# Retention in 64x64 array tiles, with the next chunk's scores inside a chunk's group and a second load of q

## The chip, the cores and the metric

One core of a Trainium2 chip runs the kernel. Its engines work side by side and wait for each other by semaphores: TensorE (PE in the profile; PEld is its loading of weights), VectorE (DVE), ScalarE (ACT), GpSimd (POOL) and SyncE (SP, which here issues the loads and stores). The metric is the device time of one execution in microseconds.

TensorE's array has 128 rows and 128 columns. A product uses as many rows as its contraction is long and as many columns as its weights have; the profile writes this shape as rows*columns. A product of 64 rows and 64 columns takes one of four such tiles, and which one follows from the partitions of its operands (rows) and of its output (columns). PSUM, where products land, has banks of 512 float32 per partition.

## What is computed

```
scores = q k^T / 8 ; ret = scores * gamma_h ** (t - s) for s <= t, else 0 ; x = ret v        # 8 batches, 8 heads, 576 tokens, 64 features a head
h = relu(x w_in) ; u, v = halves of h (512 + 512)
v_n = (v - mean) / sqrt(var + 1e-6) ; v_s = w_spatial v_n + b_spatial ; out = (u * v_s) w_out
```

The first line is the retention (the part that the change touches), the rest a gated feed-forward block that mixes the tokens with `w_spatial`.

## The kernel before

**Retention in chunks.** `retention(b)` is a generator for one batch. The 576 tokens are four chunks of 128 and a tail of 64 (chunk 4). Inside a chunk the decayed scores are applied directly; what earlier chunks contribute comes through a state of 64x64 per head. For a chunk c there are four kinds of float32 product, and in the profile each counts as two matmuls:

- `scores(c)`: k^T q per head. A pair of heads lies in the two halves of the partitions, so each product has 64 rows, 128 columns (all keys) and 128 queries: shape 64*128, named sc. DVE multiplies the result with the mask `am` (decay, and zero above the diagonal) into `at`.
- `burst(c)`, first part: the increments of the state (`ds`), k^T v for each half of the chunk: 64*64 with 64 moving columns, ox<-qkv in the profile.
- second part, for c > 0: the state times the decayed queries `qsc` (ox<-qsc,st), 64*64 with 128 columns.
- third part: `at` times v (ox<-at,qkv), contracting all 128 keys: 128*64 with 128 columns. It adds into the same output `xo` as the second part.

Then DVE adds the state's increments (`st`, with ACT's copy in chunk 0), POOL decays it by `sd`, ACT rounds `xo` to float32r (`hi`) and DVE takes the rest (`lo`): x is kept as two float32r parts, as all operands of the large products are.

**Preparation.** `prep(c)` is POOL's: k is scaled by `kd` in place, and q times `qs` goes to `qsc`. Both read the chunk's one load (`load`, 1 MB: q, k with features in partitions, k, v with tokens in partitions), issued two chunks ahead by SP after the group that frees its buffer.

**Order.** For each chunk: burst(c), load(c+2), prep(c+1), scores(c+1); a batch's first scores stand alone ahead of it. The pool `ps_r` gives scores and bursts, by turns, one of two pairs of PSUM banks.

**Main work.** The other products are float32r with 128 rows and 128 columns, three matmuls for each pair of two-part operands (`mm3`): v (512 columns), u, vs and f (288 columns). `main(b)` yields after each tile of output, and `interleave` puts a batch's retention between the tiles of the main work of the batch before, by shares that the generators yield. In the startup batch 0's retention runs with the conversion of the weights (`front`, `mid`, `back`, `w_sp_steps`, over ACT, DVE and POOL), in an order written out by hand; batch 1's retention lies in `main(0)`, together with the conversion of w_out (`convert_wout`). Up to there every engine keeps program order. After that (`ordered[0] = False`) a planner orders the instructions, except that the matmuls issued by `mm`, all of the retention's, keep their order. The `u_pair` tiles of batch 0 use the pairs of `ps_r` too.

Of the kernel before, what the change touches and what calls it, by code (L numbers as in the profile page):

```python
# [17 lines left out]
P = 128  # L18
# [12 lines left out]


@with_exitstack
def retention_gmlp(ctx, tc, qkv, qk_t, v_t, w_in, w_sp, b_sp, w_out, amask, qscale, kdec, sdec, out):
    nc = tc.nc
    cp = ctx.enter_context(tc.tile_pool(name="cp", bufs=1))
    ld = ctx.enter_context(tc.tile_pool(name="ld", bufs=2))
    wk = ctx.enter_context(tc.tile_pool(name="wk", bufs=2))
    sp = ctx.enter_context(tc.tile_pool(name="sp", bufs=1))
    ps_r = ctx.enter_context(tc.tile_pool(name="ps_r", bufs=2, space=PSUM))  # L40
    ps_m = ctx.enter_context(tc.tile_pool(name="ps_m", bufs=4, space=PSUM))

    am = cp.tile([P, 2, NP, C], F32, name="am")
# [12 lines left out]
        return cp.tile([P, 2, NCB, S], F32R, name=name, tag="slot", bufs=2)  # L56

    chunk = {}
    ordered = [True]

    class Engine:
# [28 lines left out]
    def spin(name, n):  # L90
        ps = ps_m.tile([P, 512], F32, name=name, tag="m")
        for i in range(n):
            pe.matmul(ps, idle[:, :P], idle, start=True, stop=True)

    spin("idle0", 12)

    def load(b, c):
        if b == 0 and c in (2, 3):
            tag = ("u", "wout0")[c - 2]
            t = cp.tile([P, NDB, S] if c == 2 else [P, NDB, DM], F32, name=f"qkv_{b}_{c}", tag=tag)  # L100
            t = t.rearrange("p a n -> p (a n)")[:, :4 * 512].rearrange("p (a n) -> p a n", a=4)
        else:
            t = ld.tile([P, 4, 512], F32, name=f"qkv_{b}_{c}", tag="qkv")
        q, k = (t[:, i].rearrange("p (a n) -> p a n", a=NP) for i in range(2))
        if c == NC:
            dma(t[:, :2].rearrange("p i (a n) -> p i a n", a=NP)[:, :, :, :TL], qk_t[b])
            for i in range(2):
                dma(t[i * TL:(i + 1) * TL, 3], v_t[b])
        elif (b, c) == (0, 0):
            dma(t[:, :2], qkv[b, c, :, :2])  # L110
            dma(am, amask)
            dma(kd, kdec)
            dma(t[:, 2:], qkv[b, c, :, 2:])
# [97 lines left out]
    def mm(out, w, r, start, stop):  # L211
        tc.keep_in_program_order(pe.matmul(out, w, r, start=start, stop=stop))

    def retention(b):
        at = {}
        qsc = {}
        half = [slice(i * D, (i + 1) * D) for i in range(2)]

        def rows(c):
            return C if c < NC else TL  # L220

        def scores(c):
            n = rows(c)
            q, k, _, _ = chunk[b, c]
            ps = ps_r.tile([P, 2, NP, C], F32, name=f"sc_{b}_{c}", tag="r")
            for p in range(NP):
                for i in range(2):
                    mm(ps[:n, i, p, :n] if c < NC else ps[half[i], i, p, :n], k[half[i], p, :n], q[half[i], p, :n], True, True)
            a = wk.tile([P, 2, NP, C], F32, name=f"at_{b}_{c}", tag="at")
            if c < NC:  # L230
                ve.tensor_tensor(out=a, in0=ps, in1=am, op=ALU.mult)
            else:
                for i in range(2):
                    r = half[i]
                    ve.tensor_tensor(out=a[r, i, :, :n], in0=ps[r, i, :, :n], in1=am[r, i, :, r], op=ALU.mult)
            at[c] = a

        def prep(c):
            q, _, kn, _ = chunk[b, c]
            n = rows(c)  # L240
            if c < NC:
                kh = kn.rearrange("p (h d) -> p h d", h=H)
                po.tensor_tensor(out=kh, in0=kh, in1=kd.broadcast_to([P, H, D]), op=ALU.mult)
            if c > 0:
                t = wk.tile([P, NP, C], F32, name=f"qsc_{b}_{c}", tag="qsc")
                po.tensor_tensor(out=t[:, :, :n], in0=q[:, :, :n], in1=qs[:, :, :n], op=ALU.mult)
                qsc[c] = t

        def burst(c):
            n = rows(c)  # L250
            _, _, kn, vv = chunk[b, c]
            ps = ps_r.tile([P, 2, 2, 2 * C], F32, name=f"ox_{b}_{c}", tag="r")
            ds = ps[:, :, 0].rearrange("p r (a d) -> p r a d", a=NP)
            xo = ps[:, :, 1].rearrange("p j (a n) -> p j a n", a=2)
            if c < NC:
                for p in range(NP):
                    for r in range(2):
                        for i in range(2):
                            m = i ^ r
                            hd = slice((2 * p + m) * D, (2 * p + m + 1) * D)  # L260
                            mm(ds[half[m], r, p], kn[half[r], hd], vv[half[r], hd], True, True)
            order = [(p, i) for j in range(2) for p, i in ((2 * j, 0), (2 * j, 1), (2 * j + 1, 1), (2 * j + 1, 0))]
            if c > 0:
                for p, i in order:
                    mm(xo[half[i ^ (p % 2)], i, p // 2, :n], st[c % 2][half[i], p], qsc[c][half[i], p, :n], p < 2, False)
            for p, i in order:
                h = 2 * p + i
                r = slice(0, n) if c < NC else half[i]
                mm(xo[half[i ^ (p % 2)], i, p // 2, :n], vv[r, h * D:(h + 1) * D], at[c][r, i, p, :n], c == 0, c == 0 or p >= 2)
            t = slice(c * C, c * C + n)  # L270
            hi, lo = ((xs[b][:, i, :, t] if c < NC else xt[:, :, i]).rearrange("p (a j) n -> p j a n", j=2) for i in range(2))
            src = xo[:, :, :, :n]
            if c < NC:
                new, tmp = st[(c + 1) % 2], st[2]
# [12 lines left out]

        xs[b] = slot(f"x_{b}")
        nxt = [(b, c) for c in range(NC + 1)] + [(b + 1, c) for c in range(2)]
        scores(0)  # L290
        yield 0.95
        prep(0)
        yield 0.0
        for c in range(NC + 1):
            yield from burst(c)
            if c + 2 < len(nxt) and nxt[c + 2][0] < B and nxt[c + 2] not in chunk:
                load(*nxt[c + 2])
            if c < NC:
                if b == 0:
                    yield 0.0  # L300
                prep(c + 1)
                if b == 0:
                    yield 0.0
                scores(c + 1)
            yield 2.65

    def mm3(ps, w, r, start, stop):
# [180 lines left out]
    up = {}  # L488

    def u_pair(db):  # L490
        t = ps_r.tile([P, 2, 512], F32, name=f"u_0_{db}", tag="r")
        up[db] = [t[:, i, :HALF] for i in range(2)]
        for i in range(2):
            u_mm(0, db, i, up[db][i])
# [55 lines left out]


_OUT = (B, DM, S)


def _constants():
# [5 lines left out]
    amask = np.where(rel[:, None, :] >= 0, scale * dec, 0.0)  # L561
    kdec = scale * gamma[None, :] ** (C - i)[:, None]
# [3 lines left out]
    f = lambda a: np.ascontiguousarray(a, dtype=np.float32)  # L566
    return {"amask": f(amask.reshape(C, NP, 2, C).transpose(0, 2, 1, 3)), "qscale": f(qscale), "kdec": f(kdec[..., None]), "sdec": f(sdec[..., None])}


def _layout(q, k, v, moe_w_in, moe_w_spatial, moe_b_spatial, moe_w_out):  # L570
# [10 lines left out]
        return a[..., :m].reshape(B, P, NP, NC, C).transpose(0, 3, 1, 2, 4).reshape(B, NC, P, NP * C)  # L581

    def tkc(a):
        return a[:, :m].reshape(B, NC, C, H * D)

    def heads(a):
        return a.reshape(H, D, -1)[[0, 2, 3, 1, 4, 6, 7, 5]].reshape(H * D, -1)

    c = np.ascontiguousarray
    return {  # L590
        "qkv": c(np.stack([fc(qf), fc(kf), tkc(kn), tkc(vv)], axis=3)),
        "qk_t": c(np.stack([qf[..., m:], kf[..., m:]], axis=2)),
        "v_t": c(vv[:, m:]),
        "w_in": c(heads(moe_w_in)).view(np.uint64),
        "w_sp": c(moe_w_spatial.T),
# [19 lines left out]
```

## Time and profile before

| | us |
|---|---|
| median of 3 runs | 577.2 |
| lowest, highest | 576.71, 577.96 |
| the profiled execution's own time | 577.02 |
| its span, first to last instruction | 574.9 |
| TensorE busy | 559.3 |
| VectorE busy | 273.3 |
| ScalarE busy | 208.4 |
| GpSimd busy | 126.9 |

The granted clock of TensorE was 0.99 on the mean. 56.60 MB were moved by DMA. The retention's products take 43.3 us (sc) and some 81 us (ox) of TensorE's busy time as the profile counts it; these lengths overlap where matmuls run in different tiles of the array, so the time that they occupy is read from where the next one starts. All code lines show as L69, the helper that records each operation, so groups are told apart by the names of their tiles.

### The profile page before, as it was taken

How to read it: one execution, taken by the hardware profiler on the slowest of the kernel's cores; microseconds unless marked ns; L12 is line 12 of the kernel's file. 1: busy time of each engine (PE TensorE's matmuls, PEld its weight loads, DVE VectorE, ACT ScalarE, POOL GpSimd, SP SyncE). 2: the span in 40 equal slices, each digit the busy share in tenths (PEclk: the TensorE clock that was granted, in tenths of full speed). 3: DMA queues.
4: the chain of work that ended last, by engine and by line, in shares of the span. 5: the costliest groups of instructions: out<-in, count | busy, mean ns of one | idle time of the engine just before them, and what ended most of it. 6: DMA issues, size and time to landing. Idle time of an engine off the chain costs nothing.

```text
span 574.9 us, 13265 instructions
## 1 busy us (share of the span) xinstructions
PE 559.3 (97%) x5716; PEld 510.6 (89%) x5716; DVE 273.3 (48%) x603; ACT 208.4 (36%) x451; POOL 126.9 (22%) x128
## 2 busy tenths in 40 slices
PE   7897997999999999999999999999999999999997
PEld 5677996989998899988999899998999889998997
DVE  5878667173532725157251654417353382515350
ACT  4365422264122632236222552226422362225422
POOL 4686555222001220122102220022201122000000
PEclk8999998999999999999999999999999999999999
DMA  8974222522133311432124221232213331010002
GB/s 328 368 242 138 74 77 63 204 75 74 38 114 118 91 63 42 182 108 79 38 74 157 74 75 38 95 136 74 75 38 124 107 112 59 16 63 21 2 1 83
DMA packets 29740, 56.60 MB, mean 98 GB/s; under 512 B 10737, under 2 KB 23025, under 8 KB 25714
## 3 DMA queue, kind: packets, MB, share of 16 engines
q1 hardware_dynamic: 29682, 55.76, 28.8%
q8 instruction: 45, 0.74, 0.5%
q14 instruction: 13, 0.11, 0.1%
HBM read 46.31 MB, written 9.44 MB: 97 GB/s over the span
## 4 chain that ended last, share of the span: by engine, by line
PE 85%; DVE 6%; POOL 3%; ACT 2%; issue 2%; DMA 1%; SPq 0%; ACTq 0%; POOLq 0%
PE vs L69 19%; PE f L69 17%; PE u L69 17%; PE v L69 16%; PE ox L69 10%; PE sc L69 6%; DVE f L69 2%; DMA raw_v<-in_w_in 1%; DVE w L69 1%; POOL f L69 1%; DVE at L69 1%; POOL qsc L69 1%; DVE st L69 1%; POOL qkv L69 1%; POOL wout L69 0%
## 5 line engine op out<-in xcount | busy, mean ns | idle before, releaser
L69 PE MATMUL vs<-wsp,vn 128*128 128x288 f32 x768 | 114.0, 297 | 0.0
L69 PE MATMUL u<-x,win 128*128 128x288 f32 x768 | 107.1, 299 | 3.2 <-POOL win L69 1.9
L69 PEld LDWEIGHTS u<-x,win 128*128 128x128 f32 x768 | 104.6, 191 | 5.3 <-POOL win L69 2.4
L69 PEld LDWEIGHTS vs<-wsp,vn 128*128 128x128 f32 x768 | 105.2, 188 | 1.6
L69 PE MATMUL f<-g,wout 128*128 128x288 f32 x768 | 105.4, 296 | 0.0
L69 PEld LDWEIGHTS f<-g,wout 128*128 128x128 f32 x768 | 102.7, 188 | 0.6
L69 PE MATMUL v<-win,x 128*128 128x512 f32 x384 | 94.1, 400 | 0.0
L69 PEld LDWEIGHTS v<-win,x 128*128 128x128 f32 x384 | 70.9, 188 | 17.8
L69 POOL TENSOR_TENSOR qkv<-qkv,kd 128x512 f32<-128x512 f32 x32 | 33.9, 1059 | 142.1 <-DMA qkv<-in_qkv 117.7
L69 DVE TENSOR_TENSOR at<-sc,am 128x1024 f32<-128x1024 f32 (+1 forms) x48 | 45.6, 950 | 40.4 <-PE sc L69 40.2
L69 ACT CAST g<-vs 128x288 fp32r<-128x288 f32 x64 | 25.5, 399 | 102.2 <-DVE vs L69 99.9
L69 DVE TENSOR_TENSOR st<-ox,st 128x256 f32<-128x256 f32 x56 | 23.5, 420 | 66.8 <-PE ox L69 65.5
L69 ACT COPY o<-f 128x288 f32<-128x288 f32 x64 | 25.5, 400 | 72.3 <-PE f L69 72.3
L69 POOL TENSOR_TENSOR st<-st,sd 128x256 f32<-128x256 f32 x24 | 14.7, 613 | 151.2 <-DVE st L69 151.2
L69 DVE BATCH_NORM_STATS2 s<-v 128x6 f32<-128x512 f32 (+1 forms) x40 | 27.9, 697 | 36.4 <-ACT v L69 35.5
L69 DVE TENSOR_TENSOR g<-vs,g 128x288 fp32r<-128x288 f32 x64 | 29.3, 457 | 30.3 <-ACT g L69 30.3
L69 PE MATMUL sc<-qkv 64*128 64x128 f32 (+1 forms) x640 | 43.3, 276 | 0.2 <-DMA qkv<-in_qkv 0.2
L69 PEld LDWEIGHTS sc<-qkv 64*128 64x128 f32 (+1 forms) x640 | 36.0, 180 | 7.9 <-issue 7.1
L69 DVE TENSOR_TENSOR vs<-vs,u 128x288 f32<-128x288 f32 x64 | 29.7, 464 | 26.6 <-PE vs L69 26.6
L69 ACT ACTIVATE u<-u 128x288 f32<-128x288 f32 x64 | 25.6, 407 | 44.6 <-PE u L69 44.6
L69 PE MATMUL ox<-at,qkv 128*64 128x128 f32 (+1 forms) x640 | 40.4, 274 | 0.1
L69 POOL TENSOR_TENSOR qsc<-qkv,qs 128x512 f32<-128x512 f32 (+1 forms) x32 | 36.7, 1148 | 12.0 <-DMA qkv<-in_qk_t 10.5
(64 smaller groups left out, 511.9 us busy)
## 6 DMA issues: line engine op xcount, KB each, us to landing
qkv<-in_qkv SPq DMA_DIRECT2D x31, 1024.0 KB, 5.1
out<-o SPq DMA_DIRECT2D x64, 144.0 KB, 1.8
raw_v<-in_w_in SPq DMA_DIRECT2D x4, 512.0 KB, 7.1
qkv<-in_qk_t SPq DMA_DIRECT2D x8, 256.0 KB, 3.3
qkv<-in_v_t SPq DMA_DIRECT2D x16, 128.0 KB, 3.3
raw<-in_w_in SPq DMA_DIRECT2D x4, 512.0 KB, 7.5
raw<-in_w_out SPq DMA_DIRECT2D x4, 512.0 KB, 3.4
raw_s<-in_w_sp SPq DMA_DIRECT2D x4, 288.0 KB, 8.4
```

The lines of the kernel that those rows point to most:

```text
L69: ins = op(*args, **kw)
```

## The change

- **Scores in blocks.** The products are cut by halves of the keys: the first 64 keys against all queries from there on, the second 64 keys only against the last 64 queries. Each has 64 rows and 64 columns. The block above the diagonal isn't computed; what the mask's operation reads there is left from earlier use of the bank. The two pairs of banks are cleared by memsets at the start.
- **at times v in two parts.** The first 64 queries contract 64 keys (64*64, 64 columns), the last 64 queries 128 keys (128*64, 64 columns).
- **Tiles of the array.** In odd pairs of heads the halves are exchanged (`side`): for `at`, the state, the decayed queries and the tokens of k and v of four heads (`_TURNED`). Host-side layouts and constants follow. The sequence `heads` lets four products in a row fall on the four 64x64 tiles, with the rows' half deciding the bank.
- **Order.** From batch 1 on scores(c+1) is issued inside burst(c), between the state's product and at's, and prep(c+1) ahead of the burst. The first scores of batches 2 to 7 are issued inside the tail's burst of the batch before. Batch 0 keeps its order.
- **Second load of q.** The decayed state needs q with exchanged halves, so `qsc` is loaded from an array of its own (`q_x`, 256 KB a chunk; `q_xt`, 128 KB for the tail) into its buffer right behind the chunk's load, and POOL scales it in place. In batch 0, chunk 3's uses the buffer of `vl`, and the tail's load comes after `fetch_wsp`.
- **PSUM.** The two pairs are two fixed tiles that `pair()` hands out by turns. The tail's mask is one operation instead of two.

```diff
+    banks = [ps_r.tile([P, 2, 512], F32, name=f"r{i}") for i in range(2)]
+    for t in banks:
+        ve.memset(t, 0.0)
...
+    def load_qsc(b, c):
+        t = wk.tile([P, NP, C], F32, name=f"qsc_{b}_{c}", tag="vl" if (b, c) == (0, 3) else "qsc", bufs=1 if (b, c) == (0, 3) else 2)
+        if c < NC:
+            dma(t, q_x[b, c - 1].rearrange("p (a n) -> p a n", a=NP))
+        else:
+            dma(t[:, :, :TL], q_xt[b])
+        qsc[b, c] = t
...
+    heads = [[(p, i) for p in (2 * j, 2 * j + 1) for i in range(2)] for j in range(NP // 2)]
+    heads = heads[0] + heads[1]
+
+    def side(p, i):
+        return i ^ (p % 2)
+
+    def scores(b, c):
+        n = rows(c)
+        q, k, _, _ = chunk[b, c]
+        ps = pair().rearrange("p i (a n) -> p i a n", a=NP)
+        for s in range(n // D):
+            for p, i in heads:
+                mm(ps[half[s ^ side(p, i)], i, p, s * D:n], k[half[i], p, half[s]], q[half[i], p, s * D:n], True, True)
+        a = wk.tile([P, 2, NP, C], F32, name=f"at_{b}_{c}", tag="at")
+        ve.tensor_tensor(out=a[:, :, :, :n], in0=ps[:, :, :, :n], in1=am[:, :, :, :n], op=ALU.mult)
+        at[b, c] = a
...
+        def burst(c, nx):
...
             if c > 0:
-                for p, i in order:
-                    mm(xo[half[i ^ (p % 2)], i, p // 2, :n], st[c % 2][half[i], p], qsc[c][half[i], p, :n], p < 2, False)
-            for p, i in order:
-                h = 2 * p + i
-                r = slice(0, n) if c < NC else half[i]
-                mm(xo[half[i ^ (p % 2)], i, p // 2, :n], vv[r, h * D:(h + 1) * D], at[c][r, i, p, :n], c == 0, c == 0 or p >= 2)
+                for p, i in heads:
+                    e = side(p, i)
+                    mm(xo[half[i], e, p // 2, :n], st[c % 2][half[e], p], qsc[b, c][half[e], p, :n], p < 2, False)
+            if b and nx:
+                scores(*nx)
+            for s in range(n // D):
+                for p, i in heads:
+                    h = 2 * p + i
+                    e = side(p, i)
+                    r = half[e] if s == 0 else slice(0, n)
+                    t = slice(s * D, (s + 1) * D)
+                    mm(xo[half[i], e, p // 2, t], vv[r, h * D:(h + 1) * D], at[b, c][r, i, p, t], c == 0 and s == 0 and p < 2, s == n // D - 1 and p >= 2)
...
         for c in range(NC + 1):
-            yield from burst(c)
+            nx = nxt[c + 1] if nxt[c + 1][0] < B else None
+            if b and nx:
+                prep(*nx)
+            yield from burst(c, nx)
             if c + 2 < len(nxt) and nxt[c + 2][0] < B and nxt[c + 2] not in chunk:
                 load(*nxt[c + 2])
```

More of the change, by code (lines that the diff above doesn't have):

```diff
@@ L33, in retention_gmlp @@
 @with_exitstack
-def retention_gmlp(ctx, tc, qkv, qk_t, v_t, w_in, w_sp, b_sp, w_out, amask, qscale, kdec, sdec, out):
+def retention_gmlp(ctx, tc, qkv, q_x, qk_t, q_xt, v_t, w_in, w_sp, b_sp, w_out, amask, qscale, kdec, sdec, out):
     nc = tc.nc
@@ L39, in retention_gmlp @@
     sp = ctx.enter_context(tc.tile_pool(name="sp", bufs=1))
-    ps_r = ctx.enter_context(tc.tile_pool(name="ps_r", bufs=2, space=PSUM))
+    ps_r = ctx.enter_context(tc.tile_pool(name="ps_r", bufs=1, space=PSUM))
     ps_m = ctx.enter_context(tc.tile_pool(name="ps_m", bufs=4, space=PSUM))
@@ L58, in retention_gmlp @@
     chunk = {}
+    qsc = {}
     ordered = [True]
@@ L93, in spin, with pair @@
             pe.matmul(ps, idle[:, :P], idle, start=True, stop=True)
-    spin("idle0", 12)
+    banks = [ps_r.tile([P, 2, 512], F32, name=f"r{i}") for i in range(2)]
+    for t in banks:
+        ve.memset(t, 0.0)
+    def pair():
+        banks.reverse()
+        return banks[0]
+    spin("idle0", 12)
+    def load_qsc(b, c):
[5 more added lines that the diff above has]
+        qsc[b, c] = t
     def load(b, c):
@@ L116, in load @@
         chunk[b, c] = q, k, t[:, 2], t[:, 3]
+        if c and (b, c) != (0, NC):
+            load_qsc(b, c)
     staged = {}
@@ L212, in mm @@
         tc.keep_in_program_order(pe.matmul(out, w, r, start=start, stop=stop))
-    def retention(b):
[L215 to L249, printed above, removed]
@@ new lines, in retention_gmlp, with rows @@
+    at = {}
+    half = [slice(i * D, (i + 1) * D) for i in range(2)]
+    def rows(c):
+        return C if c < NC else TL
+    heads = [[(p, i) for p in (2 * j, 2 * j + 1) for i in range(2)] for j in range(NP // 2)]
[12 more added lines that the diff above has]
+        at[b, c] = a
@@ L250, in burst, with prep @@
+    def prep(b, c):
+        n = rows(c)
+        if c < NC:
+            kh = chunk[b, c][2].rearrange("p (h d) -> p h d", h=H)
+            po.tensor_tensor(out=kh, in0=kh, in1=kd.broadcast_to([P, H, D]), op=ALU.mult)
+        if c > 0:
+            t = qsc[b, c][:, :, :n]
+            po.tensor_tensor(out=t, in0=t, in1=qs[:, :, :n], op=ALU.mult)
+    def retention(b):
+        def burst(c, nx):
             n = rows(c)
             _, _, kn, vv = chunk[b, c]
-            ps = ps_r.tile([P, 2, 2, 2 * C], F32, name=f"ox_{b}_{c}", tag="r")
+            ps = pair().rearrange("p i (a n) -> p i a n", a=2)
@@ L257, in burst @@
                     for r in range(2):
[L258 to L262, printed above, removed]
-            if c > 0:
-                for p, i in order:
-                    mm(xo[half[i ^ (p % 2)], i, p // 2, :n], st[c % 2][half[i], p], qsc[c][half[i], p, :n], p < 2, False)
-            for p, i in order:
-                h = 2 * p + i
-                r = slice(0, n) if c < NC else half[i]
-                mm(xo[half[i ^ (p % 2)], i, p // 2, :n], vv[r, h * D:(h + 1) * D], at[c][r, i, p, :n], c == 0, c == 0 or p >= 2)
+                        for e in (r, 1 - r):
+                            h = 2 * p + side(p, e)
+                            hd = slice(h * D, (h + 1) * D)
+                            mm(ds[half[e], r, p], kn[half[r], hd], vv[half[r], hd], True, True)
+            if c > 0:
+                for p, i in heads:
[10 more added lines that the diff above has]
+                    mm(xo[half[i], e, p // 2, t], vv[r, h * D:(h + 1) * D], at[b, c][r, i, p, t], c == 0 and s == 0 and p < 2, s == n // D - 1 and p >= 2)
             t = slice(c * C, c * C + n)
@@ L289, in retention @@
         nxt = [(b, c) for c in range(NC + 1)] + [(b + 1, c) for c in range(2)]
[L290 to L293, printed above, removed]
+        if (b, 0) not in at:
+            scores(b, 0)
+            yield 0.95
+            prep(b, 0)
+            yield 0.0
+        else:
+            yield 0.95
         for c in range(NC + 1):
-            yield from burst(c)
+            nx = nxt[c + 1] if nxt[c + 1][0] < B else None
+            if b and nx:
+                prep(*nx)
+            yield from burst(c, nx)
             if c + 2 < len(nxt) and nxt[c + 2][0] < B and nxt[c + 2] not in chunk:
                 load(*nxt[c + 2])
[L298 to L304, printed above, removed]
+            if b == 0 and c < NC:
+                yield 0.0
+                prep(*nx)
+                yield 0.0
+                scores(*nx)
             yield 2.65
@@ L446, in retention_gmlp @@
     fetch_wsp()
+    load_qsc(0, NC)
     back(1, 1)
@@ L490, in u_pair @@
     def u_pair(db):
-        t = ps_r.tile([P, 2, 512], F32, name=f"u_0_{db}", tag="r")
+        t = pair()
         up[db] = [t[:, i, :HALF] for i in range(2)]
@@ L552 @@
 _OUT = (B, DM, S)
+_TURNED = [h for h in range(H) if (h ^ (h // 2)) % 2]
 def _constants():
@@ L561, in _constants @@
     amask = np.where(rel[:, None, :] >= 0, scale * dec, 0.0)
+    amask[D:, :, :D] = amask[D:, :, D:]
     kdec = scale * gamma[None, :] ** (C - i)[:, None]
@@ L566, in _constants @@
     f = lambda a: np.ascontiguousarray(a, dtype=np.float32)
+    for a in (amask, kdec):
+        a[:, _TURNED] = np.roll(a[:, _TURNED], D, axis=0)
+    for a in (qscale, sdec):
+        a[:, 1::2] = np.roll(a[:, 1::2], D, axis=0)
     return {"amask": f(amask.reshape(C, NP, 2, C).transpose(0, 2, 1, 3)), "qscale": f(qscale), "kdec": f(kdec[..., None]), "sdec": f(sdec[..., None])}
@@ L583, in tkc @@
     def tkc(a):
-        return a[:, :m].reshape(B, NC, C, H * D)
+        t = a[:, :m].reshape(B, NC, 2, D, H, D)
+        t = np.stack([t[:, :, ::-1, :, h] if h in _TURNED else t[:, :, :, :, h] for h in range(H)], axis=4)
+        return t.reshape(B, NC, C, H * D)
     def heads(a):
-        return a.reshape(H, D, -1)[[0, 2, 3, 1, 4, 6, 7, 5]].reshape(H * D, -1)
+        return a.reshape(H, D, -1)[[0, 3, 2, 1, 4, 7, 6, 5]].reshape(H * D, -1)
     c = np.ascontiguousarray
+    qx = qf.copy()
+    qx[:, :, 1::2] = np.roll(qx[:, :, 1::2], D, axis=1)
     return {
         "qkv": c(np.stack([fc(qf), fc(kf), tkc(kn), tkc(vv)], axis=3)),
+        "q_x": c(fc(qx)[:, 1:]),
         "qk_t": c(np.stack([qf[..., m:], kf[..., m:]], axis=2)),
+        "q_xt": c(qx[..., m:]),
         "v_t": c(vv[:, m:]),
```

## The prediction

> **What bounds the kernel now.** I read the page first: busy shares, then the chain that ended last.
>
> ```profile
> span 574.9 us, 13265 instructions
> PE 559.3 (97%) x5716; PEld 510.6 (89%) x5716; DVE 273.3 (48%) x603; ACT 208.4 (36%) x451; POOL 126.9 (22%) x128
> PE 85%; DVE 6%; POOL 3%; ACT 2%; issue 2%; DMA 1%; SPq 0%; ACTq 0%; POOLq 0%
> ```
>
> TensorE is busy 97% of the span and is 85% of the chain. A busy PE is not a PE at its peak, so I asked next what it waits for. The waits of PE from 112 us to the end list nothing at all; before 112 us the largest entry is this one:
>
> ```profile
> PE ox L69 <- POOL qkv L69: 6.1, 3, 3.4
> ```
>
> So from batch 1's main work on (about 111 us) the time is the length of PE's own stream, and what shortens that stream shortens the span one for one. Before that, batch 0's chain goes through the conversions of weights on DVE, ACT and POOL. The two parts are costed apart.
>
> The timeline (start, length, engine, operation) shows the retention groups. Here one group of chunk 2 in the steady part, then the ends of those of chunks 3, 4 and 0, with the lone first scores:
>
> ```profile
> 211.32 0.69 PE L69 MATMUL ox<-qkv 64*64 64x64 f32 x32
> 211.84 0.62 PE L69 MATMUL ox<-qsc,st 64*64 64x128 f32 x16
> 212.38 0.85 PEld L69 LDWEIGHTS ox<-at,qkv 128*64 128x64 f32 x16 [0.17 <-issue]
> 212.39 1.09 PE L69 MATMUL ox<-at,qkv 128*64 128x128 f32 x16
> 213.41 1.16 PE L69 MATMUL sc<-qkv 64*128 64x128 f32 x16
> 214.50 1.87 PE L69 MATMUL vs<-wsp,vn 128*128 128x288 f32 x12
> ...
> 225.88 0.69 PE L69 MATMUL ox<-qkv 64*64 64x64 f32 x32
> 227.97 0.68 PE L69 MATMUL sc<-qkv 64*64 64x64 f32 x16
> 228.58 1.85 PE L69 MATMUL vs<-wsp,vn 128*128 128x288 f32 x12
> ...
> 238.81 0.46 PE L69 MATMUL ox<-qsc,st 64*64 64x64 f32 x16
> 239.09 0.41 PE L69 MATMUL ox<-at,qkv 64*64 64x64 f32 x16
> 239.44 6.67 PE L69 MATMUL f<-g,wout 128*128 128x288 f32 x48
> ...
> 246.03 1.16 PE L69 MATMUL sc<-qkv 64*128 64x128 f32 x16
> 247.13 5.88 PE L69 MATMUL v<-win,x 128*128 128x512 f32 x24
> ...
> 252.93 0.69 PE L69 MATMUL ox<-qkv 64*64 64x64 f32 x32
> 255.67 4.70 PE L69 MATMUL v<-win,x 128*128 128x512 f32 x19
> ```
>
> Read starts, not lengths: a row's length holds the drain of its last matmul. From start to start chunk 2's group is: state increments (ds) 0.52, the decayed state's product (st) 0.55, the scores' product (at) 1.02, next scores (sc) 1.09; 3.18 us in all. Each float32 product is two matmuls, hence 8 products are x16.
>
> **Unit prices from these rows.** On 64x64 tiles and 64 columns, 32 ds matmuls take 0.52 us and the 16 at 238.81 take 0.28; the difference, 0.24 us, is 16 matmuls in an open mode (a first round costs 0.04 more). The 16 at 239.09 take 0.35 up to the next shape, so leaving a mode costs 0.35 - 0.24 = 0.11. With that, st's 0.55 is 0.44 for 16 matmuls of 128 columns plus 0.11 for leaving.
>
> **The change on PE.** In the steady part a group becomes ds, st, sc, and at in two halves, all on 64x64 tiles but the last half. For a middle chunk:
> - ds 0.52 and st 0.44: it is no longer followed by a change of shape (0.11 gone).
> - sc, first half of the keys against 128 queries: 16 matmuls of st's shape, 0.44; second half against 64 queries: 16 of ds's shape, 0.24. The old 1.09 goes.
> - at, first 64 queries: 0.24 + 0.11 for leaving. At, last 64 queries: 16 matmuls of 128x64 tiles with 64 columns, a form that the trace doesn't have. By the same form with 128 columns (1.02 - 0.11 = 0.91) it costs between half and all of that, 0.46 to 0.91. I take 0.49, near the half and twice 0.24, since two tiles instead of four share the array and both forms on 64x64 tiles scaled with their columns (0.24 against 0.44). Plus 0.11 for leaving: 0.60.
>
> Sum: 0.52 + 0.44 + 0.44 + 0.24 + 0.35 + 0.60 = 2.59 against 3.18, **0.59 us saved**. Upper end of the unknown: 0.17 saved.
>
> Chunk 0 has no st: 255.67 - 252.93 = 2.74 becomes 2.59 - 0.44 = 2.15, again 0.59. Chunk 3 has the tail's scores: 228.58 - 225.88 = 2.70 becomes 0.52 + 0.44 + 0.24 + 0.35 + 0.60 = 2.15, 0.55 saved.
>
> Chunk 4 takes in the next batch's first scores. The lone group goes: 1.10 (246.03 to 247.13) plus what an interruption costs the big matmuls. The chain gives that:
>
> ```profile
> 232.56 6.32 PE f L69 x48
> 239.51 6.60 PE f L69 x48
> 559.09 12.74 PE f L69 x96
> ```
>
> Two parts are 12.92, the undivided last batch 12.74: 0.18 us. Gone are 1.28, added 0.44 + 0.24 = 0.68; 0.60 saved.
>
> From 111 us on, batches 2 to 7 run their chunks 0 to 3 (their retention lies beside the main work of the batch before), and five lone first scores go (batches 3 to 7): 6 x (3 x 0.59 + 0.55) + 5 x 0.60 = 13.9 + 3.0 = **16.9 us**.
>
> At this point I weigh a page. The Trainium skill (TensorE: Matmul & The Clock Gate, Part 3, The mechanism) says that a weight load overlaps running matmuls only where it uses another row group. The last half of at has all 128 rows in both of its tiles, so by that page it would not gain from its shorter matmuls; the row at 212.38 shows 0.85 us of such loads inside a group whose matmuls last 1.09, overlapped, so the trace so far doesn't bear the page out.
>
> **What lies beside PE.** Where one of these covers fails, PE waits in order and its delay is added:
> - Loads. 32 more on SP (three of 256 KB and a tail of 128 KB a batch), each behind the chunk's own and ahead of later stores.
>
> ```profile
> 228.12 0.33 SPq L69 DMA_DIRECT2D qkv<-in_qkv  x1
> 233.19 1.04 POOL L69 TENSOR_TENSOR qkv<-qkv,kd 128x512 f32<-128x512 f32 x1 [15.36 <-DMA qkv<-in_qkv]
> ```
>
> This chunk is used 5.1 us after its issue (POOL waits for it until then); a quarter more of bytes makes it 6.4; groups stand 11 to 15 us apart. Issue adds 0.33 each on a queue that is not in the chain. Nothing, both ends.
> - POOL's prep moves ahead of the group, so the decay of the state (st by sd) queues behind it. POOL is busy 22%, and the state is due a group later: nothing.
> - DVE's mask of the next scores now comes ahead of the state's adds; one mask of 128x512 replaces two for the tail. Sums equal, DVE 48% busy: nothing.
> - The buffers of PSUM are still two pairs; the pair for the scores was read by DVE a group ago.
>
> **Batch 0 and batch 1's retention (to 111 us).** Startup: two memsets more on DVE and 0.75 MB more ahead of the weights on SP.
>
> ```profile
> GB/s 328 368 242 138 74 77 63 204 75 74 38 114 118 91 63 42 182 108 79 38 74 157 74 75 38 95 136 74 75 38 124 107 112 59 16 63 21 2 1 83
> 4.65 1.43 DVE L69 TENSOR_SCALAR w<-w 128x512 f32<-128x512 f32 x2 [3.20 <-ACT w L69]
> 17.95 4.67 SPq L69 DMA_DIRECT2D raw<-in_w_in  x4
> 29.20 0.69 ACT L69 ACTIVATE f<-raw 128x512 f32<-128x512 f32 x1
> raw<-in_w_in SPq DMA_DIRECT2D x4, 512.0 KB, 7.5
> ...
> 65.55 1.10 PE L69 MATMUL ox<-at,qkv 128*64 128x128 f32 x16
> 68.22 0.69 DVE L69 TENSOR_TENSOR x<-ox,x 128x512 fp32r<-128x512 f32 x1 [0.71 <-ACT x L69]
> 68.83 1.21 DVE L69 TENSOR_TENSOR at<-sc,am 128x1024 f32<-128x1024 f32 x1
> ```
>
> A memset of 1024 columns costs at most what a mask of 1024 does (1.21); two fit the 3.20 us in which DVE waits. 0.75 MB at 368 GB/s (second slice) are 2.1 us: the first raw block lands at 17.95 + 7.5 + 2.1 = 27.6, before ACT takes it at 29.20. PE's saving there (two shorter products a chunk) is mostly waited away; I count 0.3 us, between 0 and 2.
>
> Then the stall before batch 1's chunk 3:
>
> ```profile
> 87.65 3.32 PE L69 MATMUL f<-g,wout 128*128 128x288 f32 x24
> 92.67 0.61 POOL L69 TENSOR_TENSOR st<-st,sd 128x256 f32<-128x256 f32 x1
> 93.24 1.04 POOL L69 TENSOR_TENSOR qkv<-qkv,kd 128x512 f32<-128x512 f32 x1
> 94.23 1.26 POOL L69 TENSOR_TENSOR qsc<-qkv,qs 128x512 f32<-128x512 f32 x1
> 95.55 0.67 PE L69 MATMUL ox<-qsc,st 64*64 64x128 f32 x16 [0.53 <-POOL qsc L69]
> 97.97 1.27 POOL L69 TENSOR_TENSOR wout<-f,wout 128x512 fp32r<-128x512 f32 x1 [2.47 <-ACT wout L69]
> 99.10 5.24 PE L69 MATMUL f<-g,wout 128*128 128x288 f32 x36
> ```
>
> PE stands from 90.97 until POOL has prepared the chunk, behind the conversions of w_out, which go by turns over DVE, ACT and POOL. What PE saves in batch 1's chunks 0 to 2 is swallowed here. What remains: first, that chain starts earlier. After chunk 0's group DVE did the state, x and only then the mask (68.83 to 70.04). Now the mask runs while PE does at, and x ends 2.3 us after the group as before (66.65 to 68.91); the group ends 0.2 later (sc is inside, 0.68; at is 0.95, not 1.02; the lone scores before it 0.26 shorter), so DVE is free at 69.1 instead of 70.0; I count 0.6. Second, POOL's prep no longer stands behind st by sd (0.57). Third, after qsc the group is 0.44 + 0.24 + 0.35 + 0.60 = 1.63 long instead of 2.18 (0.55), more at the slow pace that it had here (3.55 from 95.55 to 99.10). Together about 1.8 at 99.10. More is barred: the fourth tile of f needs wout's last part, which POOL finished at 99.24, itself earlier by the first term only. Then the merged first scores of batch 2, 0.60. With the startup's 0.3 I take **2.7**, between 0.6 and 4.
>
> **Sum.** 16.9 + 2.7 = 19.6 us. The profiled execution took 577.0 us, 0.2 under the median of the three runs and 2.1 over its span, so 577.0 - 19.6 = 557.4: I forecast **557.4 us**; its own range is 555 to 561.
>
> **Rivals.**
> 1. The last half of at keeps its old length: its weight loads are as many and as long as before, and 0.85 us of them stood in the old group. For: the form is new. Against: in the ds group such loads go four abreast with 64-column matmuls. Each of 24 groups (batches 2 to 7) loses 0.42: 10.1 us, **568**. Chance 0.10. The skill's rule on row groups would give this time.
> 2. Slower: the new scores and the first half of at get only two of the four tiles at a time. The rows show such a thing: the tail's scores at 227.97 walk two of the four 64x64 tiles and take 0.61 for 16 matmuls, where those at 239.09 take 0.35. Then sc costs 1.36 instead of 0.68 and at's first half 0.48 instead of 0.24: 0.92 lost a group against 0.59 saved, 0.33 net; with five merged scores (0.68 - 0.60 lost each) 24 x 0.33 + 0.4 = 8.3 slower, less 2.7 at the start: **583**. It decides from rounds 65% longer on. Against: the new order of heads walks the four tiles in turn, as st's does at 211.84, which holds 0.44. Chance 0.05.
> 3. The stall at 91 us dissolves: its 3.4 us and the slow pace behind it (3.55 - 2.18 = 1.4) go, less the 1.8 already counted: 3.0 more, **554**. Against: wout's last part. Chance 0.06.
> 4. It doesn't do what it says: from batch 2's retention on the planner orders what isn't pinned, and could put large matmuls into a group. Each insertion costs 0.18 and 0.11 for leaving; two in every group eat all. About **577**, no change. In the trace all groups of the steady part are unbroken. Chance 0.02.
>
> **Numbers.** Forecast 0.77. The range 553 to 568 takes in the forecast's own, rivals 1 and 3, and both ends of the last half of at. A measurement of this kernel tells 0.2% (1.2 us) from no change. Faster: 0.77 + 0.10 + 0.06 = 0.93; within: 0.02; slower: 0.05.
>
> **What the profile after should show.** Start to start in a steady group of chunk 2: ds 0.52, st 0.44, sc 0.68, at 0.35 and 0.60; a batch's period 2.9 us shorter; no lone scores from batch 2 on; no waits of PE after 108 us. Wrong would be: at's last half near 1.0 (rival 1), sc near 1.4 (rival 2), PE waiting in a group for the chunk's load (that cover failed), or no stall before batch 1's chunk 3 (rival 3).

## The result and the profile after

The median fell from 577.58 us (four runs, 576.71 to 580.18) to 561.57 us (four runs, 560.98 to 563.39): a ratio of 0.9721, with a 95% interval of 0.9682 to 0.9759. The kernel is 16.0 us faster; 557.4 us was forecast, with a range that holds the result. Timed once more among the experiments, the changed kernel had a median of 560.91 us and a ratio of 0.9690 (0.9665 to 0.9714). The profiled execution took 563.39 us, the slowest of the four.

The profile page of the changed kernel: the span, busy times by engine, the chain that ended last, and the loads of the chunks (KB each, median us from issue to landing).

```profile
span 561.6 us, 15328 instructions
PE 539.9 (96%) x6740; PEld 501.5 (89%) x6740; DVE 277.1 (49%) x597; ACT 208.3 (37%) x451; POOL 127.8 (23%) x128
PE 83%; DVE 5%; POOL 3%; DMA 3%; issue 2%; ACT 2%; SPq 1%; ACTq 0%; POOLq 0%
...
qkv<-in_qkv SPq DMA_DIRECT2D x31, 1024.0 KB, 5.3
```

TensorE still bounds the kernel, with 1024 more instructions and 19.4 us less of busy time. In the chain, DMA has gone from 1% to 3%, the first sign that something waits where nothing did.

The steady part. First the timeline of the changed kernel (start, length) at the group of chunk 2 that lies where the prediction's first group lay:

```profile
211.10 0.69 PE L70 MATMUL r<-qkv 64*64 64x64 f32 x32
211.62 0.62 PE L70 MATMUL r<-qsc,st 64*64 64x128 f32 x16
212.06 0.85 PE L70 MATMUL r<-qkv 64*64 64x128 f32 x32
212.73 1.03 PE L70 MATMUL r<-at,qkv 64*64 64x64 f32 x32
213.68 1.87 PE L70 MATMUL vs<-wsp,vn 128*128 128x288 f32 x12
```

From start to start: ds 0.52, st 0.44, sc 0.67, at 0.95 for both of its parts. 2.58 us in all, where 2.59 was forecast and 3.18 stood before. The chain of waits gives the period, from the v tile of one batch to that of the next. The kernel before:

```profile
179.12 5.81 PE v L69 x24
...
247.20 5.81 PE v L69 x24
```

and the changed kernel:

```profile
180.31 5.60 PE v L70 x24
...
245.40 5.60 PE v L70 x24
```

The period is 65.09 us instead of 68.08: 2.99 shorter, 2.92 forecast. TensorE waits for nothing after 112 us. From batch 1's v on (110.98 before and 115.05 after in the timelines) the profiled executions took 463.9 and 446.6 us: **17.4 us saved**, 16.9 forecast.

The start is where the sign was wrong: batch 1's v comes 4.07 us later here (2.3 in the profile of the repeat, 113.28), where 2.7 earlier was forecast. The waits of TensorE in the changed kernel up to 112 us (sum, times, longest) show what is new:

```profile
PE r L70 <- POOL qkv L70: 5.1, 4, 3.0
PE r L70 <- POOL qsc L70: 3.2, 4, 1.7
PE r L70 <- DVE x L70: 2.9, 1, 2.9
PE r L70 <- DMA qkv<-in_qkv: 2.2, 2, 1.6
```

Before, the wait for x was 0.2 us, that for a chunk's load 0.2 and that for the scaled q 1.1 in two. Three waits have appeared: 1.7 for qsc, 2.9 for x, 1.6 for a load. The timeline shows each with its cause. In brackets stands the idle time before a row and what ended it. The tail of batch 0:

```profile
32.51 0.58 SPq L70 DMA_DIRECT2D qsc<-in_q_xt  x1
...
38.37 0.72 POOL L70 TENSOR_TENSOR qsc<-qsc,qs 128x256 f32<-128x256 f32 x1 [1.56 <-DMA qsc<-in_q_xt]
...
39.77 4.61 PE L70 MATMUL v<-win,x 128*128 128x512 f32 x12
```

The tail's q was issued at 32.51 behind the loads of w_spatial, and POOL got it at 38.37; the tail's decayed product began at 39.15, where before it had begun at 37.37. The v tile behind it took 4.45 us up to the next one (39.77 to 44.22), where it had taken 2.93. The late q alone doesn't do that: the granted clock from 38 to 46 us was 0.79 in this profile, and in the repeat, which also waits for the tail's q (1.20 us), it was 1.00 and the tile took 2.96.

The same timeline around batch 1's chunk 2, on POOL, DVE and PE:

```profile
78.72 1.06 POOL L70 TENSOR_TENSOR qkv<-qkv,kd 128x512 f32<-128x512 f32 x1
78.80 1.26 DVE L70 TENSOR_SCALAR f<-f 128x512 int32<-128x512 int32 x1 [1.48 <-POOL f L70]
79.72 1.48 POOL L70 TENSOR_TENSOR qsc<-qsc,qs 128x512 f32<-128x512 f32 x1
80.09 2.39 DVE L70 SCALAR_TENSOR_TENSOR f<-raw,f 128x512 int32<-128x512 int32 x2
...
85.95 1.13 PE L70 MATMUL r<-qkv 64*64 64x64 f32 x32 [2.93 <-DVE x L70]
```

and the conversion of the same block of w_out by DVE in the kernel before:

```profile
77.29 0.43 DVE L69 TENSOR_SCALAR f<-f 128x512 int32<-128x512 int32 x1 [1.46 <-POOL f L69]
77.75 1.42 DVE L69 SCALAR_TENSOR_TENSOR f<-raw,f 128x512 int32<-128x512 int32 x2
```

Three operations of DVE took 1.88 us with POOL idle, and 3.68 us (78.80 to 82.48) with POOL's prep beside them. The mask, the state's adds and x stand behind them on DVE, and TensorE's group of chunk 2 writes to the pair of banks that x (85.11 to 85.80) reads.

Last the tail of batch 1, with the first scores of batch 2 inside it:

```profile
102.20 0.39 SPq L70 DMA_DIRECT2D qkv<-in_qkv  x1
...
107.56 0.90 PE L70 MATMUL r<-qkv 64*64 64x128 f32 x32 [1.62 <-DMA qkv<-in_qkv]
...
108.62 6.59 PE L70 MATMUL f<-g,wout 128*128 128x288 f32 x36
```

The chunk's load was issued at 102.20, and the group reached its scores 3.7 us later; the median landing takes 5.3.

### The profile page after: what moved, and what is told of

The parts are those of the page before. It is cut to its first block, busy times and chain, and to the rows that moved or that the text cites. A ratio compares the mean times of both kernels' runs of the same rounds, so it can differ in the third digit from the quotient of the medians.

```text
span 561.6 us, 15328 instructions
## 1 busy us (share of the span) xinstructions
PE 539.9 (96%) x6740; PEld 501.5 (89%) x6740; DVE 277.1 (49%) x597; ACT 208.3 (37%) x451; POOL 127.8 (23%) x128
## 4 chain that ended last, share of the span: by engine, by line
PE 83%; DVE 5%; POOL 3%; DMA 3%; issue 2%; ACT 2%; SPq 1%; ACTq 0%; POOLq 0%
PE vs L70 20%; PE f L70 17%; PE v L70 17%; PE u L70 16%; PE r L70 13%; DVE f L70 3%; DMA raw_v<-in_w_in 1%; DMA raw_s<-in_w_sp 1%; DMA qkv<-in_qkv 1%; POOL f L70 1%; SPq L70 1%; POOL win L70 1%; POOL wout L70 1%; DVE w L70 1%; POOL qkv L70 0%
## 5 line engine op out<-in xcount | busy, mean ns | idle before, releaser
L70 PE MATMUL u<-x,win 128*128 128x288 f32 x672 | 91.8, 296 | 0.0
L70 PEld LDWEIGHTS u<-x,win 128*128 128x128 f32 x672 | 90.1, 188 | 1.0
L70 PEld LDWEIGHTS v<-win,x 128*128 128x128 f32 x384 | 72.2, 191 | 16.9
L70 DVE TENSOR_TENSOR at<-r,am 128x1024 f32<-128x1024 f32 (+1 forms) x40 | 44.5, 1112 | 80.5 <-PE r L70 80.3
L70 POOL TENSOR_TENSOR qsc<-qsc,qs 128x512 f32<-128x512 f32 (+1 forms) x32 | 37.1, 1158 | 194.4 <-DMA qsc<-in_q_x 123.7
L70 PEld LDWEIGHTS r<-qkv 64*64 64x64 f32 x2176 | 46.9, 138 | 19.2 <-POOL qkv L70 6.5
L70 PE MATMUL r<-qkv 64*64 64x64 f32 (+1 forms) x2176 | 53.3, 238 | 10.2 <-POOL qkv L70 5.1
L70 ACT CAST x<-r 128x512 fp32r<-128x512 f32 x32 | 18.8, 586 | 56.5 <-DVE st L70 56.3
L70 PE MATMUL r<-at,qkv 64*64 64x64 f32 (+1 forms) x1152 | 37.6, 228 | 0.0
L70 ACT ACTIVATE u<-u 128x288 f32<-128x288 f32 x56 | 22.4, 408 | 32.1 <-PE u L70 32.0
L70 PEld LDWEIGHTS r<-at,qkv 64*64 64x64 f32 (+1 forms) x1152 | 32.1, 141 | 2.3
```

Source lines behind the costliest of these rows:

```text
L70: ins = op(*args, **kw)
```

## The experiments

Each kernel was timed beside the kernel before on the same chip (medians 577.7 to 578.5 us). Diffs are against the changed kernel.

**Which edit costs the start?** Four kernels, each with one suspect taken away (a1 takes two, the order around the groups and the merged scores). `a1_old_order_b1` gives batch 1 the old order, with prep and scores behind each group:

```diff
-            if b and nx:
+            if b > 1 and nx:
...
-            if b == 0 and c < NC:
+            if b <= 1 and c < NC:
...
```

> The changed kernel with batch 1's retention alone in the old order (group, load, prep, scores; batch 2's first scores alone), blocks and tiles kept. Theory: in the changed kernel the start is lost in batch 1, by the new order of POOL's and DVE's queues (PE waits 2.9 us for x before chunk 2) and by batch 2's first scores coming before their load (1.6 us). Then neither wait is there, the old one before chunk 3 (3.4 us) is back in part, v of batch 1 starts at 112 to 113 us instead of 115.0, and the time is about 559. Rival (the start is lost in batch 0, by loads and the tail's q): v starts where it did, 115, and the time is 561.6 or, for the unmerged scores, 562.

`a2_prep_late_b1` moves only POOL's prep behind the group, in batch 1 alone:

```diff
-            if b and nx:
+            if b > 1 and nx:
                 prep(*nx)
             yield from burst(c, nx)
...
+            if b == 1 and nx:
+                prep(*nx)
```

> Only POOL's prep in batch 1 goes back behind the group; scores stay inside. Theory (prep run earlier lies beside DVE's conversions of w_out and slows them): DVE's three conversion operations before chunk 2 take 1.9 us again instead of 3.7, PE's wait for x before chunk 2 falls from 2.9 to about 1.2, time 560. Rival (the order of DVE's own queue, mask ahead of state and x, is what makes x late): the wait stays at 2.5 or more, time 561.6.

`a3_tail_q_early` issues the tail's q of batch 0 right behind the tail's own load, ahead of w_spatial, into a buffer of its own:

```diff
+        if (b, c) == (0, NC):
+            t = wk.tile([P, NP, TL], F32, name="qsc_t", tag="qsc_t", bufs=1)
...
+    load_qsc(0, NC)
...
-    load_qsc(0, NC)
```

> Only the load of q for batch 0's tail is put ahead of the weights' loads, into a buffer of its own. Theory (it lands late, behind w_spatial): POOL's wait of 1.6 us and PE's of 1.7 before the tail go, the v tile behind is back to 2.7 us from 4.2, wtl's conversion moves from 62.9 to about 61.5, time 560.5. Rival (covered by the conversions of w_in): the tail moves but nothing after 62 us, time 561.6.

`a4_lone_scores_b2` lets the first scores of batch 2 stand alone again:

```diff
-            nx = nxt[c + 1] if nxt[c + 1][0] < B else None
+            nx = nxt[c + 1] if nxt[c + 1][0] < B and (b, c) != (1, NC) else None
```

> Only batch 2's first scores stand alone again, not inside batch 1's tail group. Theory (there they wait for a load issued 3 us before): PE's wait of 1.6 us and the slow clock behind it (f in 6.3 us instead of 4.8) go, the lone group costs 0.6, time 559.3. Rival (wait hidden, slow clock comes from the earlier stalls): f stays slow, time 561.6 or 562.2.

| | median us | ratio to before | v of batch 1 at |
|---|---|---|---|
| changed, first | 561.57 | 0.9721 (0.9682 to 0.9759) | 115.05 |
| changed, repeat | 560.91 | 0.9690 (0.9665 to 0.9714) | 113.28 |
| a1, old order | 560.05 | 0.9694 (0.9676 to 0.9713) | 110.30 |
| a2, prep late | 560.33 | 0.9701 (0.9685 to 0.9717) | 111.90 |
| a3, tail's q early | 560.46 | 0.9703 (0.9688 to 0.9717) | 112.03 |
| a4, scores alone | 560.06 | 0.9696 (0.9681 to 0.9710) | 111.72 |

By its time alone none of the four can be told from the changed kernel: the intervals overlap. By their traces each removes its own wait and leaves the others, though a shorter one can take its place. In a1 the wait for x is gone, and the stall before chunk 3 grows back to 3.8 us, with the group at 94.40 as in the kernel before (94.33). With prep late, the timeline of a2 has DVE's conversion back at its old length:

```profile
78.59 0.43 DVE L70 TENSOR_SCALAR f<-f 128x512 int32<-128x512 int32 x1 [1.49 <-POOL f L70]
79.06 1.42 DVE L70 SCALAR_TENSOR_TENSOR f<-raw,f 128x512 int32<-128x512 int32 x2
...
84.15 0.69 PE L70 MATMUL r<-qkv 64*64 64x64 f32 x32 [1.33 <-POOL qkv L70]
```

and x is done at 83.79 instead of 85.80. TensorE's wait before chunk 2 fell from 2.93 to 1.33 us, and what ends it now is POOL's own late prep. In a3's timeline POOL no longer waits for the tail's q, and the tail starts 1.26 us earlier than in the changed kernel's first profile and 1.09 earlier than in the repeat:

```profile
37.89 0.46 PE L70 MATMUL r<-qsc_t,st 64*64 64x64 f32 x16 [0.64 <-DVE x L70]
```

while its waits for x (2.94) and for the load (1.90) stay. In a4's timeline the tail's group has no wait, and the lone scores cost 0.83 us (to v at 111.72):

```profile
105.56 0.41 PE L70 MATMUL r<-at,qkv 64*64 64x64 f32 x16
105.90 5.06 PE L70 MATMUL f<-g,wout 128*128 128x288 f32 x36
110.89 0.90 PE L70 MATMUL r<-qkv 64*64 64x128 f32 x32
```

**Do the three repairs add up?** `c1_old_b1_tailq` joins a1 and a3; `c2_late_lone_tailq` joins a2, a3 and a4.

> a1 and a3 together: old order in batch 1, tail's q early with its own buffer. Theory: both savings add (1.5 and 1.1), v of batch 1 starts at about 110.3, time 559.0. Rival (batch 0's delay is swallowed again at the conversions of w_out before chunk 3): as a1, 560.

> a2, a3 and a4 together: scores stay inside batch 1's groups, prep behind them, batch 2's first scores alone, tail's q early. Theory: the savings of 1.2, 1.1 and 1.5 add in the main, time 558.5. Rival (one wait takes another's place before chunks 2 and 3, since x stays behind the mask on DVE): 560.

c1: 559.09 us, ratio 0.9674 (0.9646 to 0.9702). c2: **557.87 us** (557.25 to 558.42), ratio 0.9645 (0.9622 to 0.9668), the fastest of all kernels run, 3.0 under the repeat of the changed kernel (560.14 to 561.66; the runs don't overlap, the ratios' intervals touch at their ends). In c2's timeline TensorE still waits for POOL's prep before chunks 2 and 3, and v of batch 1 is 1.0 us ahead of the kernel before:

```profile
83.84 0.69 PE L70 MATMUL r<-qkv 64*64 64x64 f32 x32 [1.32 <-POOL qkv L70]
...
95.42 0.69 PE L70 MATMUL r<-qkv 64*64 64x64 f32 x32 [1.46 <-POOL qkv L70]
...
109.97 2.37 PE L70 MATMUL v<-win,x 128*128 128x512 f32 x9
```

So the three late covers hold most of what the start lost, and they can be mended without giving up the new order from batch 2 on.

**Is the early mask to blame as well?** The prediction counted on the mask ahead of the state's adds, yet in batch 1 it stands ahead of the x that TensorE waits for. `d1_mask_late_b1` moves it behind x, in batch 1; `d2_late_lone_tailq_mask` does so on top of c2; `d3_changed_again` is the changed kernel itself.

```diff
-                scores(*nx)
+                mask = scores(*nx, late=b == 1)
...
+            if b == 1 and nx:
+                mask()
```

> The changed kernel, but in batch 1 DVE's mask of the next scores comes behind state and x, as before the change; TensorE's order and POOL's prep stay as changed. Theory (x is late through two things of one size: conversions slowed by prep 1.8 us, mask ahead 1.2): TensorE's wait for x before chunk 2 falls from 2.9 to about 1.7, time 560.8. Rival (only the slowed conversions count; the mask is made up for later): wait 2.5 or more, time 561.6.

> c2 with the mask behind state and x in batch 1 as well: DVE, POOL and the loads then work in batch 1 in their old order, and only TensorE's groups are new. Theory: the wait before chunk 2 that c2 still has (1.3 us between the last vs and the group) falls under 0.5, time 557.2. Rival (the mask then holds up the next vs tile and with it the conversions of w_out, as c2's wait before chunk 3 shows): nothing gained, 557.9 or slower.

> The changed kernel once more, unaltered. The slow f behind batch 2's first scores (6.3 us instead of 4.8) and the later first weights (1.1 us) in its first profile: if they belong to the kernel, they are there again and the median is 561.6; if they are of that execution, f takes 4.8, v of batch 1 starts near 113 and the median is still about 561.5, since medians leave that execution out.

d1 took 562.46 us, ratio 0.9722 (0.9704 to 0.9741), 1.5 more than d3; d2 took 559.43, ratio 0.9671 (0.9651 to 0.9691), 1.6 more than c2. The ratios' intervals overlap in both pairs, but the runs don't (562.19 to 563.11 against 560.14 to 561.66, 559.03 to 560.49 against 557.25 to 558.42). The timeline of d1, after the group of chunk 0 that ends at 68.70, shows DVE idle before the adds:

```profile
69.22 0.42 DVE L70 TENSOR_TENSOR st<-r,st 128x256 f32<-128x256 f32 x1 [1.07 <-ACT st L70]
...
72.10 0.45 DVE L70 TENSOR_TENSOR vs<-vs,u 128x288 f32<-128x288 f32 x1
```

and in d3's, after the group that ends at 68.22, the mask fills that gap:

```profile
67.59 1.22 DVE L70 TENSOR_TENSOR at<-r,am 128x1024 f32<-128x1024 f32 x1
...
70.48 0.46 DVE L70 TENSOR_TENSOR vs<-vs,u 128x288 f32<-128x288 f32 x1
```

The adds follow there at 68.74 with no idle time. DVE comes to the next tile (vs) 3.40 us after the group in d1 and 2.26 in d3. From chunk 0's group to chunk 3's there are 31.14 us in d1 and 30.40 in d3, 29.93 in d2 and 29.26 in c2: the late mask costs 0.7 of the 1.5 and 1.6 us there in both pairs. TensorE's wait for x before chunk 2 is still 2.57 us in d1, where 1.7 was expected, so the mask is little of what makes x late. The early mask is a gain; moving it back isn't a repair.

**What carries the steady gain?** `b1_order_old_all` keeps the blocks and tiles but puts every batch in the old order; `b2_at_whole` leaves out the division of at times v for chunks 0 to 3, so that its output also takes in the block above the diagonal.

```diff
-            if b and nx:
-                scores(*nx)
...
-            if b and nx:
-                prep(*nx)
...
-            if b == 0 and c < NC:
+            if c < NC:
...
```

> Blocks, tiles and second load kept, but the old order in every batch: prep and scores behind the group, a batch's first scores alone. Theory (rows of the changed kernel: a change of shape costs 0.11 and a first round 0.04, a lone group 0.18 more): a middle group is 2.74 us instead of 2.58, the lone scores cost 0.35 more than merged ones, a batch's period is 66.05 us instead of 65.10. The order thus carries 0.95 of the 2.98 saved a batch, the blocks 2.03. Batch 1 loses its two new waits as in a1. Time about 565.5. Rival (the order carries half or more): period 66.6 or longer, time 569 or more.

```diff
-            for s in range(n // D):
-                for p, i in heads:
...
+            for p, i in heads:
...
+                r = slice(0, n) if c < NC else half[e]
+                mm(xo[half[i], e, p // 2, :n], vv[r, h * D:(h + 1) * D], at[b, c][r, i, p, :n], c == 0 and p < 2, p >= 2)
```

> Only at times v is undivided again, 128 keys by 128 queries, one shape 128*64. The output then takes in keys above the diagonal (what the mask's operation left there). Theory by rows: undivided 0.91 + 0.11 = 1.02 from start to start, divided 0.35 + 0.61 = 0.96, so a group is only 0.06 to 0.08 longer; period 65.4 us; time about 563. Rival (the divided product carries its share by work, a quarter less): 0.25 a group, period 66.1, time 567.5.

b1: 565.29 us, ratio 0.9772 (0.9750 to 0.9794), period 66.09. Of the 2.99 us a batch, the order carries 1.00 and the blocks and tiles 1.99. The timeline of b1 shows where:

```profile
210.66 0.90 PE L70 MATMUL r<-qkv 64*64 64x128 f32 x32
211.49 1.86 PE L70 MATMUL vs<-wsp,vn 128*128 128x288 f32 x12
```

The same scores take 0.83 us behind the last part of at, and 0.67 inside the group: one more change of shape and a first round. Four such groups a batch make 0.64 of the 1.00; the other 0.36 are left for the first scores, which stand alone again. Six batches are 6.0 us; b1's median lies only 3.7 above the changed kernel's, since in batch 1 the old order is the faster one (a1): there b1 reached batch 1's v at 111.26, the repeat of the changed kernel at 113.28.

b2: 565.35 us, ratio 0.9779 (0.9753 to 0.9805), period 65.80: dividing at saves 0.71 a batch. Its timeline:

```profile
210.48 0.85 PE L70 MATMUL r<-qkv 64*64 64x128 f32 x32
211.26 1.09 PE L70 MATMUL r<-at,qkv 128*64 128x128 f32 x16
212.28 1.87 PE L70 MATMUL vs<-wsp,vn 128*128 128x288 f32 x12
```

At takes 1.02 as in the kernel before, but sc takes 0.78 up to it, not 0.67: the change of shape now falls in front of at. The group is 2.75 instead of 2.58 us long. The expected period of 65.4 had left that change out. Six batches of 0.71 are 4.3 us; b2's median is 3.8 above the changed kernel's.

**Do the four tiles have to be walked in turn?** `f1_two_tiles` takes the heads in an order in which products in a row fall on two of the four tiles:

```diff
-    heads = [[(p, i) for p in (2 * j, 2 * j + 1) for i in range(2)] for j in range(NP // 2)]
+    heads = [[(p, i) for p in (j, j + 2) for i in range(2)] for j in range(NP // 2)]
```

> The changed kernel with one line altered: heads are walked 0, 2, 1, 3 by pairs instead of 0, 1, 2, 3, so that products in a row fall on two of the four 64x64 tiles by turns, then on the other two; work and shapes are the same (at's last half, on two tiles anyway, is not touched by it). Theory (rival 2 of the prediction as a mechanism: only the sequence lets four tiles run at once): the products on 64x64 tiles but ds take twice as long, a batch gains 0.92 + 2 x 1.36 + 0.92 + 1.16 = 5.7 us, period 70.8, longer than before the change (68.1), time about 596. Rival (TensorE overlaps tiles whatever the sequence within a few products): period 65.1, time 561.

566.13 us, ratio 0.9805 (0.9787 to 0.9823), period 65.88, far nearer to the changed kernel (65.09) than to the 70.8 of two tiles at a time. The timeline of f1, in a group of chunk 2 and at the end of one of chunk 3:

```profile
211.33 0.97 PE L70 MATMUL r<-qkv 64*64 64x128 f32 x32
212.14 1.08 PE L70 MATMUL r<-at,qkv 64*64 64x64 f32 x32
213.15 1.86 PE L70 MATMUL vs<-wsp,vn 128*128 128x288 f32 x12
...
225.71 0.23 PE L70 MATMUL r<-at,qkv 64*64 64x64 f32 x2
225.72 0.22 PE L70 MATMUL r<-qkv 64*64 64x64 f32 x2
```

sc takes 0.81 (0.67 with the four in turn), at 1.01 (0.95). The last two matmuls of the scores start at 225.72, behind two of at at 225.71 that were issued after them: a matmul that was issued later started first.

## Why the prediction was right and wrong

**The steady part was right, in mechanism and size.** The unit prices taken from starts held to 0.01 us for each step of a group, and 17.4 us were saved where 16.9 were forecast. It rests on TensorE having no wait there, before and after.

**The last half of at (rival 1) was rightly set low.** Had it kept its length, at would have taken 1.37 us; it took 0.95. In the single records of the trace its second part starts at 213.07 and vs at 213.68, so it took 0.61 us with the change of shape, where 0.60 was forecast. The Trainium skill (TensorE: Matmul & The Clock Gate, Part 3, The mechanism), as the prediction read it, would have given the rival's time; the 0.95 us of this trace speak against its rule that weight loads overlap only across row groups, for this form. The same section also lets a load go ahead of running matmuls into the background weight buffer; with that the trace doesn't disagree.

**Rival 2 didn't happen**, and f1 shows that it was priced too high: even with two tiles in a row the loss is 0.79 us a batch. That products overlap in whatever tile is free is how the rows of f1 read, with later matmuls ahead of earlier ones; it wasn't tested by itself. sc took 0.81 us there, where the rival, priced from the tail's scores of the kernel before (0.61 for 16), had 1.36.

**Rival 3 didn't happen.** The stall before batch 1's chunk 3 stayed: 0.69 us behind a stretch in which the granted clock was 0.66 (82 to 92 us), and 3.25 in the repeat, where that stretch ran at 1.00. In both that group starts when POOL has prepared the chunk. In these two profiles the stall takes in what TensorE's slow pace loses: chunk 2's group came 0.60 us earlier in the repeat than in the first, and chunk 3's 0.61. The repeat's timeline, with the wait in batch 1's tail below it:

```profile
95.37 1.04 POOL L70 TENSOR_TENSOR qkv<-qkv,kd 128x512 f32<-128x512 f32 x1
...
96.47 0.69 PE L70 MATMUL r<-qkv 64*64 64x64 f32 x32 [3.25 <-POOL qkv L70]
...
107.32 0.90 PE L70 MATMUL r<-qkv 64*64 64x128 f32 x32 [1.24 <-DMA qkv<-in_qkv]
```

**The step that failed is "Batch 0 and batch 1's retention"**, with the covers costed at nothing. Its terms ahead of chunk 3's group, at 94.33 before, are 0.3, 0.6 and 0.57, some 1.5 us earlier; the group came 2.1 later in the repeat and 2.8 in the first profile. In parts:

- *"0.75 MB more ahead of the weights".* I asked whether the weights would be late behind the new loads, and not whether a new load would be late behind the weights. The tail's q is: POOL waits 1.56 us, and a3 takes that away. The first weights are late as well, and no experiment here touches that (see Open).
- *"POOL's prep moves ahead of the group ... nothing."* The busy share (22%) was the reason, and it is an average over a steady part where POOL has time. In batch 1 the moved prep meets DVE's conversion of w_out and makes it 1.8 us longer; a2 undoes this. The trace before had the price in it, at the stall before chunk 3 (its group is the first row). There the same operation of DVE ran beside POOL's qsc (94.23 to 95.49) and took 1.41 us instead of 0.43, to 0.29 after POOL's end:

```profile
94.33 0.69 PE L69 MATMUL ox<-qkv 64*64 64x64 f32 x32 [3.36 <-POOL qkv L69]
94.37 1.41 DVE L69 TENSOR_SCALAR f<-f 128x512 int32<-128x512 int32 x1
```

The Trainium skill (SBUF — State Buffer, Who interferes with whom) says that some operations of DVE share a port with GpSimd and that whichever comes second waits until the other is done. The trace agrees roughly: POOL's operation ran from 78.72 to 79.78, and DVE's, begun at 78.80 and 0.43 us long by itself, ended at 80.06, 0.28 after it.

- *"The pair for the scores was read by DVE a group ago"* and *"groups stand 11 to 15 us apart".* Both take the spacing of the steady part, and the first looks at the scores' pair alone: the pair that comes late is the group's own, which x reads. In batch 1 the groups of chunks 1 and 2 start 11.4 us apart with the wait and 8.4 without it (9.0 in the kernel before, 73.45 to 82.40), and less than 4 lie between the issue of batch 2's first load and its use. There both covers are gone: 2.93 us for x, 1.62 (1.24 in the repeat) for the load. The merged scores, forecast as 0.60 saved, cost this wait in that one place; a4 removes it.
- *The early mask*, counted as 0.6 gained, was right in its sign: d1 and d2 undo it and lose 1.5 and 1.6 us, 0.7 of it between the groups of chunks 0 and 3.

From chunk 3's group to batch 1's v there were 16.65 us before, 16.81 in the repeat, 14.83 in a4 and 14.55 in c2. In a4 and c2 batch 2's first scores don't wait for their load, and the group itself runs at full pace: 2.90 us from 95.42 to f in c2, 4.77 before (94.33 to 99.10), at a granted clock of 1.00 and 0.83 from 92 to 102 us.

So the sum of 19.6 became 17.4 saved and, by the medians, about 1.4 lost: 16.0. c2 gives back most of the difference: 557.87 us. Of the 2.7 forecast for the start c2 has 1.0; what it still waits for are chunks 2 and 3, which POOL prepares behind the conversions (1.32 and 1.46 us). The range held although the start had the wrong sign, because the start is small beside the steady part: it moved the sum by 4.1 us one way, the steady part by 0.5 the other.

**Open.** Why d2 waits 4.0 us for POOL before chunk 3, where c2 waits 1.46, was argued from DVE's gap and not tried. What a stall costs behind it can't be read from one profile. The first profile of the changed kernel ran f at 6.59 us behind its wait of 1.62, with a granted clock of 0.76 from 108 to 115 us; a2 ran the same f at 5.06 behind a wait of 1.64, with 1.00. From 82 to 92 us the granted clock was 0.66 in the first profile, 0.83 in a3 and 1.00 in the repeat, all with the same wait of 2.9 us for x, and 0.83 in a2 and c2 with one of 1.3. No run here says when the clock falls. The first weights, too, are later with the change: ACT gets them at 5.05 to 5.51 us in all 13 profiles of kernels with it, and at 3.99 in the one before, though SP issues that load at 0.72 or 0.73 in all of them. The first v tile starts at 22.37 to 23.62 there and at 21.94 before. So a part of the late start lies ahead of the three covers, and no run says what delays this load. These 13 profiles differ by 1.25 us at the first v tile, so v of batch 1 in a single profile carries about that much noise.

## What to carry to other kernels

A cover that is read from the steady part holds there: for every step that an edit moves or adds, look at the place where the work stands closest together (here, batch 1's retention), and price it by that place's rows. Ask of a new load both what it delays and what delays it. For TensorE, prices taken from the starts of rows, with the change of shape as a term of its own, gave each step of a group to 0.01 us.

## What was not expected of the hardware

- Three operations of DVE beside POOL's two products took 3.68 us instead of 1.88. The last two of them, 1.42 us long by themselves, ended 1.28 us after POOL's second product did (81.20), about as if they had waited for it.
- A change of shape cost TensorE 0.11 us at each place where these rows show one; b2 moved one from between at's two parts to ahead of at, at the same price.
- Products of 128 rows and 64 columns with 64 moving columns cost about half of those with 128: at's second part took some 0.50 us for 16 matmuls without the change of shape, where 16 with 128 columns had 0.91.
- Matmuls in different tiles can start out of the order of issue (225.71 before 225.72 in f1), which fits how little the order of heads matters (0.79 us of a period of 65); that it is the reason wasn't shown.
